# Batch 0 exchanged on the PE array instead of through DRAM, filter loads in one queue, and a new step plan for batches 1 to 7

## The chip, the cores and the metric

The kernel runs on one core of a Trainium2 chip. The metric is the device time of one execution in microseconds (us). Executions of one kernel on one chip mostly agree within about 1% (1.5% at most here); all comparisons below are between runs in the fast state, except where a run was made only once and its state is therefore unknown, which is said there.

## The reference

The input `x` (8 batches of 3072 rows and 256 channels) is filtered along its rows by a product in frequency space. The result goes through a max-out layer and an output projection.

```python
X = np.fft.rfft(x, axis=1)                       # x: 8 x 3072 x 256
y = np.fft.irfft(X * (filt_r + 1j * filt_i), n=3072, axis=1)
h = np.maximum(y @ w1, y @ w2)                   # w1, w2: 256 x 1024
out = h @ w_out                                  # w_out: 1024 x 256
```

The kernel does the transforms as matmuls, with 3072 = 128 x 24, in these stages for each batch:

- `f1`: a 128-point transform, `pa <- xb, C1`, evicted by ACT to `at`.
- an exchange of the partition axis with the 24 other rows: `at` is written to the DRAM tile `ad` and read back as `bt` (1.5 MB).
- `f2`, in eight groups: `px <- U, bt`, the product with the filter `F` on the DVE (`pq`), and `pz <- VP/VQ, pq`, evicted by ACT to `zt`.
- a second exchange through the DRAM tile `zd`, read back as `zr` in two halves.
- `s4` (`py <- zr, G1`), then the max-out layer (`ph`, `gt`) and the projection (`po`, `ot`), in 48 tiles of 8 steps each.

## The kernel before

Batch 0's transform stands before the loop of 384 steps (the setup). The transforms of batches 1 to 7 are put between the loop's steps by a plan. Max-out is computed as relu(y(w1-w2)) plus the linear part y w2 w_out, whose matrix `M` comes from `prep_w`.

```python
    def f1(b, c):
        ...
        TE.matmul(pa, C1, xb[b, c // 2][:, 2 * (c % 2):2 * (c % 2) + 2], start=True, stop=True)
        S.activation(at[:, 2 * (c % 2):2 * (c % 2) + 2], pa, AF.Copy)
        if c % 2 == 1:
            nc.sync.dma_start(out=ad[b][:, 2 * c - 2:2 * c + 2], in_=at)
    # ... setup ...
    load_f(8, 16, 0); load_f(8, 16, 1)             # written on two lines there
    G.memset(F[32:64, :, :, 0:8], 0.0)
    uu, mk = tables_u()
    for c in range(12):
        f1(0, c)
    f1_read(0)
    copy_f(8, 16, 0)
    copy_f(8, 16, 1)
    G.tensor_copy(hold, bt[0][0:1, 0:T:16, 0:1])   # POOL waits for bt here
    load_f(1, 8, 0)
    load_f(0, 8, 1)
    # ... f2 of batch 0, load_w, z_read(0, 1), prep_wd, z_read(0, 0), prep_w ...

    plan_f1(0, 1, range(3, 15), 17)     # f1 of batch 1 at these steps, its bt read at 17
    plan_x(0, 2, range(20, 48, 3))      # loads of x
    plan_f2(0, list(range(22, 39)), 33, 41)   # f2 of batch 1, zr halves read at 33 and 41
    # ... batches 2 to 4 ...
    for b in range(3, B):
        if b + 1 < B:
            plan_f2(b, list(range(0, 34, 2)), 19, 36)
        if b + 2 < B:
            plan_f1(b, b + 2, range(1, 25, 2), 28)
        if b + 3 < B:
            plan_x(b, b + 3, range(5, 48, 4))
```

## Time and profile before

The median of the first three runs was 601.76 us (600.74 to 604.93). The profiled execution took 596.9 us:

| Stage | from, to (us) | what bounds it |
|---|---|---|
| setup: batch 0's transform, weights | 0 to 82.4 (first `ph`) | transfers; PE busy 34.5 of 82.4 us |
| loop: 48 tiles, transforms of batches 1 to 7 | 82.4 to 592.5 (last store issued) | PE, busy 479.1 of 510.1 us, and waits for transfers |

The page of before cuts the span into 40 slices; each digit is the busy share of an engine in tenths, and `PEclk` is the granted TensorE clock.

```profile
PE   4415479797799998899699989998999989999996
ACT  5304237474466774575267646664676546555441
PEclk9955589899799999799799999999999999999998
DMA  8989466956369879669966974798147913551112
```

The first five slices are the setup: the DMA engines are busy, the PE hardly is, and its granted clock is 0.50 to 0.52 from 30 to 70 us. (The leading 9s of `PEclk` have no clock record behind them, the first record starts at 27.0 us: back-to-back 512-column matmuls at 23 to 27 us start 0.43 us apart, against 0.22 in the loop.)

The timeline of the DVE in the setup of before (start, duration, what; in brackets the idle time before it and what ended it):

```profile
39.87 3.48 DVE L402 TENSOR_TENSOR pq<-px,F 112x1024 bf16<-112x1024 f32 x3 [15.13 <-DMA F<-in_filt_r_dram]
...
56.77 0.60 DVE L259 TENSOR_SCALAR F<-F,e 48x256 bf16<-48x256 f32 x2
```

The first filter product waits 15 us for `F`. The second line is a small fix of the filter's first rows, 0.60 us for two instructions.

The list of what the PE waited for in the loop of before (total us, times, longest):

```profile
PE py L421 <- DMA zr<-zd: 18.9, 6, 6.2
PE pa L338 <- DMA xb<-in_x_dram: 5.0, 3, 4.2
PE px L392 <- DMA bt<-ad: 3.9, 3, 1.9
```

That is 27.8 us of idle PE. The clock records of the trace add 26.5 us at half clock inside the loop: the last 2.6 us of a stretch that began in the setup, and four stretches of 3.4 to 6.8 us that begin in or just after the longer of these waits (at 112.3, 149.8, 238.6 and 289.8 us).

The groups of before that evict `f1` and `f2` on ACT (count, busy us, mean ns of one):

```profile
L377 ACT ACTIVATE zt<-pz 112x512 bf16<-112x512 f32 x128 | 69.4, 595 | 72.0 <-PE pz L373 67.3
L339 ACT ACTIVATE at<-pa 128x512 bf16<-128x512 f32 x96 | 57.0, 600 | 35.4 <-PE pa L338 33.1
```

A 512-element eviction took 0.6 us (595 and 600 ns).

### The profile page before, as it was taken

To read this page: it belongs to the slowest core of one execution; us is meant where nothing else is said; L and a number is where in the kernel's file an instruction comes from. 1 tells how busy PE (TensorE), PEld (TensorE's weight loads), DVE (VectorE), ACT (ScalarE), POOL (GpSimd) and SP (SyncE) were. 2 spreads that over 40 slices of the span, in tenths; PEclk is the share of its full clock that TensorE was granted. 3 is DMA by queue.
4 is the path that set the end of the run, shared out by engine and by line. 5 is a ranking of instruction groups with operands and counts; after the bars stand their busy time and mean duration, and the time that the engine had idled before them with its cause. 6 is when DMAs were issued, how large, how long until landed. Compare 5 with 4: busy or idle time off the path is not lost.

```text
span 596.9 us, 11529 instructions
## 1 busy us (share of the span) xinstructions
PE 513.6 (86%) x4829; PEld 341.0 (57%) x4829; DVE 318.8 (53%) x415; ACT 324.5 (54%) x592; POOL 97.9 (16%) x148
## 2 busy tenths in 40 slices
PE   4415479797799998899699989998999989999996
PEld 0203236465466665566366656665666666677774
DVE  9426023493238736474177637773677467734342
ACT  5304237474466774575267646664676546555441
POOL 9863520110011001112011101110000000000000
PEclk9955589899799999799799999999999999999998
DMA  8989466956369879669966974798147913551112
GB/s 192 182 131 258 108 130 184 198 126 168 97 164 232 185 234 167 149 165 255 178 168 169 233 179 133 183 217 209 75 140 196 223 41 110 130 150 71 72 51 92
DMA packets 77736, 94.71 MB, mean 159 GB/s; under 512 B 5282, under 2 KB 57140, under 8 KB 76660
## 3 DMA queue, kind: packets, MB, share of 16 engines
q1 hardware_dynamic: 60196, 54.16, 39.4%
q0 software_dynamic: 17488, 39.81, 27.4%
q8 instruction: 38, 0.62, 0.4%
q14 instruction: 14, 0.11, 0.1%
HBM read 56.72 MB, written 50.33 MB: 179 GB/s over the span
## 4 chain that ended last, share of the span: by engine, by line
issue 52%; PE 21%; DMA 9%; POOL 5%; ACT 1%; DVE 0%; SPq 0%; POOLq 0%
PE ph L437 7%; PE po L462 7%; DMA zr<-zd 3%; DMA zd<-zt 3%; DMA xb<-in_x_dram 3%; POOL out_dram L468 3%; PE pa L338 2%; PE po L457 2%; PE pz L373 1%; POOL xb L89 1%; PE px L392 1%; PE py L421 1%; POOL Wd L302 1%; ACT zt L377 1%; POOL pq L402 0%
## 5 line engine op out<-in xcount | busy, mean ns | idle before, releaser
L442 ACT ACTIVATE gt<-ph 128x512 bf16<-128x512 f32 x298 | 176.3, 599 | 109.5 <-PE ph L437 108.7
L462 PE MATMUL po<-Wo,gt 128*128 128x256 bf16 x1536 | 232.9, 275 | 0.0
L462 PEld LDWEIGHTS <-gt 128*128 128x128 bf16 x1536 | 151.9, 99 | 60.1 <-issue 2.4
L402 DVE TENSOR_TENSOR pq<-px,F 112x1024 bf16<-112x1024 f32 x124 | 145.9, 1218 | 68.3 <-PE px L392 49.3
L464 DVE COPY ot<-po 128x512 f32<-128x512 f32 x96 | 66.0, 687 | 92.5 <-PE po L462 92.1
L377 ACT ACTIVATE zt<-pz 112x512 bf16<-112x512 f32 x128 | 69.4, 595 | 72.0 <-PE pz L373 67.3
L468 POOL DMA_DIRECT2D out_dram<-ot x48 | 25.8, 538 | 462.8 <-DVE ot L464 452.5
L437 PEld LDWEIGHTS <-Wd 128*128 128x128 bf16 x768 | 69.7, 99 | 29.5 <-issue 14.6
L440 DVE TENSOR_SCALAR gt<-ph 128x512 bf16<-128x512 f32 x86 | 59.0, 687 | 40.4 <-PE ph L437 32.4
L339 ACT ACTIVATE at<-pa 128x512 bf16<-128x512 f32 x96 | 57.0, 600 | 35.4 <-PE pa L338 33.1
L373 PE MATMUL pz<-pq,VP 48*64 48x256 bf16 x512 | 38.5, 288 | 30.6 <-DVE pq L402 15.2
L338 PE MATMUL pa<-xb,C 128*128 128x512 bf16 x96 | 38.6, 415 | 13.5 <-DMA xb<-in_x_dram 13.3
L421 PE MATMUL py<-G,zr 128*128 128x128 bf16 x384 | 30.4, 223 | 21.6 <-DMA zr<-zd 21.3
L421 PEld LDWEIGHTS <-zr 128*128 128x128 bf16 x384 | 25.6, 100 | 25.7 <-DMA zr<-zd 17.0
L373 PEld LDWEIGHTS <-VP 48*64 48x64 bf16 x512 | 19.1, 112 | 35.8 <-issue 32.9
L373 PE MATMUL pz<-pq,VQ 48*64 48x256 bf16 x512 | 36.7, 288 | 0.0
L392 PE MATMUL px<-bt,U 48*64 48x256 bf16 x512 | 29.7, 294 | 4.9 <-DMA bt<-ad 4.9
L89 POOL DMA_DIRECT2D xb<-in_x_dram x48 | 26.0, 555 | 0.7 <-issue 0.3
L392 PEld LDWEIGHTS <-U 48*64 48x64 bf16 x512 | 12.2, 110 | 17.9 <-issue 12.7
L338 PEld LDWEIGHTS <-C 128*128 128x128 bf16 x96 | 9.4, 101 | 21.1 <-DMA xb<-in_x_dram 10.9
L373 PEld LDWEIGHTS <-VQ 48*64 48x64 bf16 x512 | 18.7, 113 | 0.0
L402 POOL TENSOR_TENSOR pq<-xs,F 112x1024 bf16<-112x1024 f32 x4 | 8.5, 2136 | 4.1 <-ACT xs L401 2.8
(338 smaller groups left out, 525.8 us busy)
## 6 DMA issues: line engine op xcount, KB each, us to landing
out_dram<-ot POOLq DMA_DIRECT2D x48, 512.0 KB, 3.9
xb<-in_x_dram POOLq DMA_DIRECT2D x48, 256.0 KB, 6.7
ad<-at SPq DMA_DIRECT2D x48, 256.0 KB
bt<-ad SPq DMA_DIRECT2D x32, 384.0 KB
zd<-zt SPq DMA_DIRECT2D x64, 192.0 KB
zr<-zd SPq DMA_DIRECT2D x16, 768.0 KB
F<-F SPq DMA_DIRECT2D x6, 192.0 KB
w1f<-in_moe_w_dram SPq DMA_DIRECT2D x1, 1024.0 KB
```

What stands on the lines that cost most here:

```text
L338: TE.matmul(pa, C1, xb[b, c // 2][:, 2 * (c % 2):2 * (c % 2) + 2], start=True, stop=True)
L339: S.activation(at[:, 2 * (c % 2):2 * (c % 2) + 2], pa, AF.Copy)
L373: TE.matmul(pz[c][64 * k:64 * k + 64, i], W[64 * c:64 * c + 48, 2 * g + i, k], pq[k][64 * c:64 * c + 48, ri, i], start=(ri == 0), stop=(ri ...
L377: S.activation(zt[0:ROWS, c, o:o + 2], pz[c][0:ROWS], AF.Copy)
L392: TE.matmul(px[k][64 * c:64 * c + 64, i], U[64 * k:64 * k + 48, t_], bt_[64 * k:64 * k + 48, t_], start=True, stop=True)
L402: E.tensor_tensor(pq[k][0:ROWS], src[0:ROWS].rearrange("p (o i) d -> p o i d", o=1).to_broadcast([ROWS, 2, 2, D]), F[0:ROWS, :, k, 2 * g:2 ...
L421: TE.matmul(py[:, n], zr[b][:, 4 * i + n, 128 * dc:128 * dc + 128], G1, start=True, stop=True)
L437: TE.matmul(ph, Wd[:, dc, 128 * j:128 * j + 128], y_[:, dc].rearrange("p a b -> p (a b)"), start=(dc == 0), stop=(dc == 1))
L440: V.tensor_scalar(gt[tt][:, j], ph, 0.0, None, OP.max)
L442: S.activation(gt[tt][:, j], ph, AF.Relu)
L462: TE.matmul(p_, g_[:, jj, 128 * n:128 * n + 128], Wo[:, jj], start=False, stop=(jj == 7))
L464: V.tensor_copy(ot[tt][:, n - 1:n + 1], po[tt])
```

## The change

The intent: batch 0 has nothing to overlap with, so its two exchanges through DRAM stand open in the setup. The PE array can transpose instead: `f1` of batch 0 is computed with channels on partitions (`At`), transposed to `bt`, and after `f2`, which now also leaves channels on partitions (`Zt`), transposed again to `zr`. With no `bt` to wait for, all loads of `F` go out behind the loads of `x` without holds or memsets. `prep_w` moves into the loop, and batches 1 to 7 get new steps, counted over the whole loop.

```diff
+    def first_s1(c):
+        for dh in range(2):
+            pa = ps.tile([128, 4, 128], FP32, tag="ps", name="pa")
+            for n in range(4):
+                TE.matmul(pa[:, n], xb[0, c][:, n, 128 * dh:128 * dh + 128], C1, start=True, stop=True)
+            S.activation(At[:, dh, :, 4 * c:4 * c + 4].rearrange("p k n -> p n k"), pa, AF.Copy)
+    def first_t1(g, engines):      # transposes At to bt
...
+    def first_s3(g, pq, Zt):
+        ...                        # 32 matmuls of 48 columns into pz
+            S.activation(Zt[:, :, :, k0:k0 + 8].rearrange("p h n k -> p h k n"),
+                         pz[c].rearrange("p h i k (a n) -> p h (i k a) n", a=2), AF.Copy)
+    def first_t2(j, engine, Zt):   # transposes Zt to zr
...
-    G.memset(F[32:64, :, :, 0:8], 0.0)
-    for c in range(12):
-        f1(0, c)
-    f1_read(0)
-    G.tensor_copy(hold, bt[0][0:1, 0:T:16, 0:1])
...
+    plan(5, prep_w)
+    plan_f1(1, spaced(2, 1, 12), 15)
+    plan_f2(1, spaced(21, 2.5, 9), 34, 43)
...
+    plan_f1(3, spaced(68, 2, 12), 92)
+    plan_f2(3, spaced(98, 4, 9), 117, 132)
+    plan_x(4, spaced(88, 4, 6))
+    plan_f1(4, spaced(110, 2, 12), 134)
+    plan_f2(4, spaced(142, 4.5, 9), 163, 180)
+    for n in range(5, B):
+        o = 48 * (n - 5)
+        plan_x(n, spaced(124 + o, 4, 6))
+        plan_f1(n, spaced(148 + o, 2, 12), 172 + o)
+        plan_f2(n, spaced(182 + o, 5, 9), 204 + o, 224 + o)
```

`spaced(first, gap, count)` lists steps; the last numbers of a `plan_f1` and a `plan_f2` line are the steps of the `bt` read and of the two `zr` reads.

More of the change, by code (lines that the diff above doesn't have):

```diff
@@ L78 @@
     zrpool = ctx.enter_context(tc.tile_pool(name="zrpool", bufs=2))
+    late = ctx.enter_context(tc.tile_pool(name="late", bufs=1))
+    w2b = late.tile([128, 2, HID], BF16)
+    w2T = late.tile([128, 8, D], BF16)
     setup = ExitStack()
@@ L116, in copy_f @@
                               in_=F[64 * c:64 * c + 24, ri, :, u0:u1])
-    F0 = init.tile([48, 2, 2, D], FP32)
+            if c == 0:
+                nc.sync.dma_start(out=F[48:64, ri, :, u0:u1], in_=F[0:16, ri, :, u0:u1])
+    F0 = init.tile([64, 2, 2, D], FP32)
     def load_f0():
         for ri, f in enumerate((filt_r, filt_i)):
-            for q in range(2):
-                for dr in range(2):
-                    src = bass.AP(f.tensor, f.offset + 64 * dr * D, [[128 * D, J], [(96 - 128 * dr) * D, 2], [1, D]])
-                    if dr:
-                        src = bass.AP(f.tensor, f.offset + 64 * D, [[128 * D, J], [-32 * D, 2], [1, D]])
-                    p0 = 24 * q + 12 * dr
-                    nc.sync.dma_start(out=F0[p0:p0 + 12, ri], in_=src)
+            for p0, n in ((0, J), (12, J), (24, J), (36, J), (48, J), (60, 4)):
+                if p0 % 24 == 0:
+                    src = bass.AP(f.tensor, f.offset, [[128 * D, n], [96 * D, 2], [1, D]])
+                else:
+                    src = bass.AP(f.tensor, f.offset + 64 * D, [[128 * D, n], [-32 * D, 2], [1, D]])
+                nc.sync.dma_start(out=F0[p0:p0 + n, ri], in_=src)
     def patch_f0():
@@ L156 @@
            allow_small_or_imprecise_dtypes=True)
-    G.memset(F[32:64, :, :, 8:16], 0.0)
     V.memset(I128, 0.0)
@@ L223, in tables_u @@
         ub = init.tile([128, 2, 2, J], FP32)
-        uu = init.tile([128, 2, T, 2, J], FP32)
-        ru = init.tile([128, 2, T, 2, J], FP32)
+        ur = init.tile([128, 2, 2, T, 2, J], FP32, tag="uz", name="ur")
+        uu, ru = ur[:, 0], ur[:, 1]
         for q in range(2):
@@ L258, in fix_f @@
         for ri in range(2):
-            V.tensor_scalar(F[0:48, ri, 0, 0], F0[:, ri, 0], e0[0:48, ri:ri + 1], None, OP.mult)
-        V.tensor_copy(F[0:48, :, 1, 0], F0[:, :, 1])
+            V.tensor_scalar(F[0:64, ri, 0, 0], F0[:, ri, 0], e0[0:64, ri:ri + 1], None, OP.mult)
+        V.tensor_copy(F[0:64, :, 1, 0], F0[:, :, 1])
     def tables_pe():
@@ L281, in tables_pe @@
                 V.tensor_copy(VQ[:, 4 * k:4 * k + 4], pw)
-    w1f = init.tile([128, 2, HID], FP32)
-    w2f = init.tile([128, 2, HID], FP32)
-    w2b = init.tile([128, 2, HID], BF16)
-    w2T = init.tile([128, 8, D], BF16)
     def load_w():
-        nc.sync.dma_start(out=w1f, in_=moe_w1.rearrange("(c p) j -> p c j", p=128))
-        nc.sync.dma_start(out=w2f, in_=moe_w2.rearrange("(c p) j -> p c j", p=128))
+        w1f = init.tile([128, 2, 2, HID], FP32, tag="aw", name="wf")
+        for i, w in enumerate((moe_w1, moe_w2)):
+            G.dma_start(out=w1f[:, i], in_=w.rearrange("(c p) j -> p c j", p=128))
+        return w1f[:, 0], w1f[:, 1]
     def spin(n):
@@ L296, in spin, with prep_wd @@
             TE.matmul(pd, SW, VP[:, 0:4].rearrange("p u b n -> p (u b n)"), start=True, stop=True)
-    def prep_wd():
+    def prep_wd(w1f, w2f):
         for dc in range(2):
@@ L386, in gen_f2 @@
         made = []
-        for n, g in enumerate((4, 5, 6, 7, 2, 3, 1, 0)):
+        for g in (4, 5, 6, 7, 2, 3, 1, 0):
             px = [ps.tile([128, 2, D], FP32, tag="ps", name="px") for _ in range(2)]
@@ L396, in gen_f2 @@
                 pq.append(pqpool.tile([128, 2, 2, D], BF16, tag="pq", name="pq"))
-                E, src = V, px[k]
-                if b == 0 and k == 1 and n in (1, 3, 4, 6):
-                    E = G
-                    src = init.tile([128, 2, D], FP32, tag="xs", name="xs")
-                    S.activation(src[0:ROWS], px[k][0:ROWS], AF.Copy)
-                E.tensor_tensor(pq[k][0:ROWS],
-                                src[0:ROWS].rearrange("p (o i) d -> p o i d", o=1).to_broadcast([ROWS, 2, 2, D]),
+                V.tensor_tensor(pq[k][0:ROWS],
+                                px[k][0:ROWS].rearrange("p (o i) d -> p o i d", o=1).to_broadcast([ROWS, 2, 2, D]),
                                 F[0:ROWS, :, k, 2 * g:2 * g + 2], OP.mult)
@@ L411, in gen_f2 @@
         yield
+    def first_s1(c):
[5 more added lines that the diff above has]
+    def first_t1(g, engines):
+        for c in range(2):
+            t0 = 8 * (g // 2) + 4 * c + 2 * (g % 2)
+            pt = ps.tile([128, 2, D], FP32, tag="ps", name="pt")
+            for i in range(2):
+                for dh in range(2):
+                    k0 = 24 * 4 * (t0 + i)
+                    a_ = At[:, dh].rearrange("p k n -> p (k n)")
+                    TE.matmul(pt[0:64, i, 128 * dh:128 * dh + 128], a_[:, k0:k0 + 64], I128, start=True, stop=True)
+                    TE.matmul(pt[64:112, i, 128 * dh:128 * dh + 128], a_[:, k0 + 48:k0 + 96], I128,
+                              start=True, stop=True)
+            if engines[c] == "v":
+                V.tensor_copy(bt[0][0:ROWS, t0:t0 + 2], pt[0:ROWS])
+            else:
+                S.activation(bt[0][0:ROWS, t0:t0 + 2], pt[0:ROWS], AF.Copy)
@@ new lines, in first_s2 @@
+    def first_s2(g, pool):
+        px = [ps.tile([128, 2, D], FP32, tag="ps", name="px") for _ in range(2)]
+        for i in range(2):
+            for k, c in QUADS:
+                t_ = 8 * (g // 2) + 4 * c + 2 * (g % 2) + i
+                TE.matmul(px[k][64 * c:64 * c + 64, i], U[64 * k:64 * k + 48, t_],
+                          bt[0][64 * k:64 * k + 48, t_], start=True, stop=True)
+        pq = []
+        for k in range(2):
+            pq.append(pqpool.tile([128, 2, 2, D], BF16, tag="pq", name="pq"))
+            E, src = V, px[k]
+            if k == 1 and pool:
+                E = G
+                src = init.tile([128, 2, D], FP32, tag="xs", name="xs")
+                S.activation(src[0:ROWS], px[k][0:ROWS], AF.Copy)
+            E.tensor_tensor(pq[k][0:ROWS],
+                            src[0:ROWS].rearrange("p (o i) d -> p o i d", o=1).to_broadcast([ROWS, 2, 2, D]),
+                            F[0:ROWS, :, k, 2 * g:2 * g + 2], OP.mult)
+        return pq
@@ new lines, in first_s3 @@
+    def first_s3(g, pq, Zt):
+        pz = [ps.tile([128, 2, 2, 2, 48], FP32, tag="ps", name="pz") for _ in range(2)]
+        for dh in range(2):
+            for i in range(2):
+                for k in range(2):
+                    for ri, W in enumerate((VP, VQ)):
+                        for c in range(2):
+                            TE.matmul(pz[c][:, dh, i, k], pq[k][64 * c:64 * c + 48, ri, i, 128 * dh:128 * dh + 128],
+                                      W[64 * c:64 * c + 48, 2 * g + i, k, 0:48], start=(ri == 0), stop=(ri == 1))
+        for c in range(2):
+            k0 = 4 * (8 * (g // 2) + 4 * c + 2 * (g % 2))
+            S.activation(Zt[:, :, :, k0:k0 + 8].rearrange("p h n k -> p h k n"),
+                         pz[c].rearrange("p h i k (a n) -> p h (i k a) n", a=2), AF.Copy)
@@ L413 @@
+    def first_t2(j, engine, Zt):
+        pt = ps.tile([128, 2, D], FP32, tag="ps", name="pt")
+        for n in range(2):
+            for dh in range(2):
+                TE.matmul(pt[:, n, 128 * dh:128 * dh + 128], Zt[:, dh, 2 * j + n], I128, start=True, stop=True)
+        if engine is V:
+            V.tensor_copy(zr[0][:, 2 * j:2 * j + 2], pt)
+        else:
+            S.activation(zr[0][:, 2 * j:2 * j + 2], pt, AF.Copy)
     yt = {}
@@ L438, in moe_h @@
                       y_[:, dc].rearrange("p a b -> p (a b)"), start=(dc == 0), stop=(dc == 1))
-        if j in (1, 5) and not (tt < 12 and 20 <= 8 * (tt % 6) + j < 40):
+        if j in (1, 5) and not in_f2(8 * tt + j):
             V.tensor_scalar(gt[tt][:, j], ph, 0.0, None, OP.max)
@@ L478 @@
     load_f(8, 16, 1)
-    G.memset(F[32:64, :, :, 0:8], 0.0)
-    uu, mk = tables_u()
-    for c in range(12):
-        f1(0, c)
-    patch_f0()
-    f1_read(0)
-    copy_f(8, 16, 0)
-    copy_f(8, 16, 1)
-    hold = init.tile([1, 2, 1], BF16)
-    G.tensor_copy(hold, bt[0][0:1, 0:T:16, 0:1])
     load_f(1, 8, 0)
     load_f(0, 8, 1)
-    load_wo()
+    At = init.tile([128, 2, 128, N2], BF16, tag="aw", name="At")
+    bt[0] = bpool.tile([128, T, D], BF16, tag="bt", name="bt")
+    for c in range(6):
+        first_s1(c)
+    uu, mk = tables_u()
+    patch_f0()
+    for c in range(2):
+        copy_f(8, 16, c)
     copy_f(1, 8, 0)
     copy_f(0, 8, 1)
+    first_t1(4, "vv")
+    first_t1(5, "vv")
     sines_u(uu, mk)
     tables_pe()
-    spin(8)
-    f2 = gen_f2(0)
-    for n in range(8):
-        if n == 7:
-            fix_f()
-        next(f2)
-        if n == 2:
-            load_w()
-        if n == 5:
-            z_read(0, 1)
-            prep_wd()
-    drain(f2)
-    z_read(0, 0)
-    prep_w()
-    spin(16)
+    Zt = init.tile([128, 2, N2, 128], BF16, tag="uz", name="Zt")
+    for g in (6, 7, 2, 3, 1, 0):
+        first_t1(g, "sv")
+    wf = load_w()
+    load_wo()
+    pend = None
+    for n, g in enumerate((4, 5, 6, 7, 2, 3, 1, 0)):
+        if n == 6:
+            fix_f()
+        pq = first_s2(g, n in (0, 2, 3, 5))
+        if pend:
+            first_s3(*pend, Zt)
+        pend = g, pq
+        if n == 4:
+            prep_wd(*wf)
+    first_s3(*pend, Zt)
+    zr[0] = zrpool.tile([128, N2, D], BF16, tag="zr", name="zr")
+    for c in range(6):
+        load_x(1, c)
+    for j in range(4):
+        first_t2(j, (V, S)[j % 2], Zt)
+    for j in range(4, 12):
+        first_t2(j, (V, S)[j % 2], Zt)
     setup.close()
@@ L515, with plan, plan_x, plan_f1 @@
     opool = ctx.enter_context(tc.tile_pool(name="opool", bufs=2))
-    keep = ctx.enter_context(tc.tile_pool(name="keep", bufs=1))
-    hold = keep.tile([1, 2, 1], BF16)
-    G.tensor_copy(hold, zr[0][0:1, 0:2, 0:1])
-    for c in range(6):
-        load_x(1, c)
     s4(0)
     todo = {}
-    def plan(b, step, fn, *a):
-        todo.setdefault((b, step), []).append((fn, a))
-    def plan_f1(b, nb, steps, read):
-        for c, n in zip(range(12), steps):
-            plan(b + n // 48, n % 48, f1, nb, c)
-        plan(b + read // 48, read % 48, f1_read, nb)
-    def plan_f2(b, steps, z1, z0):
+    def plan(step, fn, *a):
+        todo.setdefault(step, []).append((fn, a))
+    def plan_x(n, steps):
+        for c, s_ in enumerate(steps):
+            plan(s_, load_x, n, c)
+    def plan_f1(n, steps, read):
+        for c, s_ in enumerate(steps):
+            plan(s_, f1, n, c)
+        plan(read, f1_read, n)
+    def plan_f2(n, steps, z1, z0):
         g = []
@@ L540, in go, with spaced, in_f2 @@
             if not g:
-                g.append(gen_f2(b + 1))
+                g.append(gen_f2(n))
             next(g[0], None)
-        for n in list(steps[1:16:2]) + [steps[16]]:
-            plan(b, n, go)
-        plan(b, z1, z_read, b + 1, 1)
-        plan(b, z0, z_read, b + 1, 0)
-    def plan_x(b, nb, steps):
-        for c, n in zip(range(6), steps):
-            plan(b, n, load_x, nb, c)
-    plan_f1(0, 1, range(3, 15), 17)
-    plan_x(0, 2, range(20, 48, 3))
-    plan_f2(0, list(range(22, 39)), 33, 41)
-    plan_f1(1, 2, range(0, 12), 15)
-    plan_x(1, 3, range(17, 48, 3))
-    plan_f2(1, list(range(20, 37)), 31, 39)
-    plan_f1(1, 3, range(38, 50), 53)
-    plan_x(2, 4, range(7, 40, 3))
-    plan_f2(2, [n for n in range(9, 48) if n % 3], 23, 37)
-    plan_f1(2, 4, [n for n in range(14, 48) if n % 3], 41)
-    plan_x(2, 5, range(26, 48, 4))
-    for b in range(3, B):
-        if b + 1 < B:
-            plan_f2(b, list(range(0, 34, 2)), 19, 36)
-        if b + 2 < B:
-            plan_f1(b, b + 2, range(1, 25, 2), 28)
-        if b + 3 < B:
-            plan_x(b, b + 3, range(5, 48, 4))
+        for s_ in steps:
+            plan(s_, go)
+        plan(z1, z_read, n, 1)
+        plan(z0, z_read, n, 0)
+    def spaced(first, gap, count):
+        return [first + int(gap * i) for i in range(count)]
+    plan(5, prep_w)
+    plan_f1(1, spaced(2, 1, 12), 15)
+    plan_f2(1, spaced(21, 2.5, 9), 34, 43)
+    plan_x(2, spaced(16, 2.5, 6))
+    plan_f1(2, spaced(31, 1.2, 12), 46)
+    plan_f2(2, spaced(57, 3, 9), 71, 83)
+    plan_x(3, spaced(50, 3, 6))
+    plan_f1(3, spaced(68, 2, 12), 92)
[8 more added lines that the diff above has]
+        plan_f2(n, spaced(182 + o, 5, 9), 204 + o, 224 + o)
+    def in_f2(step):
+        return 20 <= step < 43 or 57 <= step < 83 or 98 <= step < 132
     for tt in range(6 * B + 1):
@@ L574 @@
         for j in range(8):
-            step = 8 * i + j
+            step = 8 * tt + j
             if tt < 6 * B:
@@ L579 @@
                 moe_o(tt - 1, j)
-            for fn, a in todo.get((b, step), ()):
+            for fn, a in todo.get(step, ()):
                 fn(*a)
```

## The prediction

> **What bounds it now.** Two stages. Setup (batch 0's transform, weights) lasts until the first `ph` matmul at 82.4 us (timeline). The TensorE is mostly idle there (windows: 0 us busy in 30-40, 1.7 in 60-70), its clock 0.5 from 30 to 75 us; it waits for transfers. The DVE waits 15.1 us for `F` (to 39.9): its loads are held back behind two 7 us POOL memsets and a `hold` copy that waits for `bt` (31.0). POOL waits 5.6 us for `w2f`, so its last `pq` is done at 68.3 and the PE waits 11 us for it. Then zd write 3.3 and zr read 5.8 us stand in the chain, until 81.2.
> The loop (82.4 to 592.5, 510 us) is PE-bound: a plain tile takes 8.2 us, one with transform work about 10.9, so I estimate 48*8.2+7*10.5 = 467 us, so some 40 us are stalls: `zr` waits 18.9 us, `xb` 5.0, `bt` 3.9 (list of waits), each long one followed by 3.4 to 6.8 us at half clock (windows: 0.67 to 0.83 near 110, 150, 240, 290).
>
> **What the change does, costed.**
> Removed in setup: four DRAM crossings of batch 0 (1.5 MB each), both memsets (13.9 us POOL; the first also held the DVE), holds, spins.
> Added on PE: 128 + 48 transposes at about 0.12 us on half clock (the 16 `w2b` transposes took 1.89 us): `t2` 5.7 us, `t1` 6 to 11; `s3` becomes 256 narrow matmuls. Evictions: 16 for `t1`, 12 for `t2`, about 0.65 us each, shared by DVE and ACT.
> New chain, estimated: x landed 13.5; `At` 15; tables 21; `t1` until 28-31. `F` loads queue right behind x: twelve at 0.57 us each on POOL, so the half for the first groups lands near 20, its copies near 25-28. First `pq` near 31 (39.9 before). Groups at 2.3 us. The weights' buffer is shared with `At`, so they load only after `t1` and land near 40; casts and subtraction (2.0+4.6 us POOL) still precede POOL's last `pq`, near 50. Then `t2`, `s4`: first `ph` near 63 (58 to 70). Gain about 18 us.
> Moved: `prep_w` into the loop (step 5): +3 us, before hidden behind the zr read.
>
> **Loop.** x(4) is issued about 20 steps before use: the 4.2 us stall at 237-241 and its cold clock go, -7. The last group of batches 5 to 7 comes 16 steps before its `py` (14 before): three waits of about 2 us go, -6. Batch 3: same distance, less bunched, -3. Against: batch 1's last group comes at step 41, not 38, before a `py` at 47: its zr wait (6.2 us) grows, +2. Sum -11 with prep_w.
>
> [...] The new setup stays mostly at half clock.
>
> **Predicted: 573 us, 8 in 10 between 560 and 588.** Faster by over 2%: 0.92; within 2%: 0.07; slower: 0.01.
>
> **What would show it.** First `pq` before 34 us; first `ph` at 58-70; no ad/zd traffic for batch 0; PE waits for POOL `pq` before `t2`; the longest loop wait is `zr` of batch 1; no `xb` wait over 1 us; no `zr` wait in batches 5 to 7.
>
> **What would make it wrong.** `F` copies or weights landing late because everything shares one queue; narrow `s3` or `t1` costing more at half clock; batch 1's or 2's zr wait growing past 10 us.

About 18 us in the setup and 11 in the loop, off the 602 us of before, give the 573. What the trace of before shows is clock records of 3.41 us and multiples of it, at half clock for 44.4 us in the setup and for 3.4 to 6.8 us in or just after the longer waits of the loop. "Mostly at half clock" was the estimate for the new setup; in the changed kernel the records show half clock from 49.8 to 83.9 us and do not begin before 43.0.

## More of the kernel before

The timeline of the SP queue of before, around the end of one batch in the steady part of the loop:

```profile
394.18 0.98 SPq L382 DMA_DIRECT2D zd<-zt  x2
396.78 5.36 SPq L348 DMA_DIRECT2D bt<-ad  x4
402.18 3.31 SPq L382 DMA_DIRECT2D zd<-zt  x2
412.03 0.45 SPq L355 DMA_DIRECT2D zr<-zd  x1
```

The `zr` read must wait until the last `zd` writes have landed (in the loop of before the SP queue waits 70.4 us for `zd` ahead of its `zr` reads, in 22 waits). Here it goes 6.5 us after the last of them was issued (402.18+3.31 to 412.03). Just ahead of them stand four issues that read the next batch's `bt`.

## The result

The changed kernel took 624.89 us (median of 4, 622.9 to 626.01) against 603.02 for before on the same chip: a ratio of 1.036, 95% interval 1.031 to 1.041. It is slower. Ratios here and below are the mean time of one kernel's runs over that of the other's of the same rounds, so they are not quite the ratio of the medians quoted. Executions over 1.5% slower than the fastest of the same kernel are left out of the means. The profiled executions, 624.2 and 596.9 us, differ by a little more than the medians do.

| (us, from the profiles) | before | after | predicted |
|---|---|---|---|
| first `pq` on the DVE | 39.9 | 45.3 | 31 |
| first `ph` (end of setup) | 82.4 | 86.1 | 63 |
| first `ph` to the last store | 510.1 | 533.7 | 499 |

So both halves of the prediction failed: the setup is 3.7 us longer, not 19 shorter, and the loop 23.6 us longer, not 11 shorter.

The same lines of the page of after:

```profile
PE   3164379898899959994899969996799989999996
ACT  7977977486367727781476527663377545555541
PEclk9995589899799979998899979999799989999999
DMA  9955513967976795678647954688445943341112
```

The DMA engines are indeed less busy in the setup (slices 3 to 6 add up to 16 tenths, where before they add up to 27), but ACT is now the engine that is busy there. Its groups show why:

```profile
L463 ACT ACTIVATE Zt<-pz 128x384 bf16<-128x384 f32 x16 | 28.2, 2110 | 5.8 <-PE pz L459 5.8
L414 ACT ACTIVATE At<-pa 128x512 bf16<-128x512 f32 x12 | 28.3, 2835 | 2.2 <-PE pa L413 2.2
```

The twelve `At` evictions have the shape of the old 0.6 us ones and take 28.3 us together, one every 2.36 us (the mean of one, 2.8 us, includes the overlap with its neighbour). The sixteen of `Zt` take 28.2 us. At 0.6 us each, all 28 would be about 17 us; some 40 us of ACT time were added, on the chain that leads to `ph`. The timeline of the PE where the setup ends:

```profile
80.27 4.58 PE L470 MATMUL pt<-I,Zt 128*128 128x128 bf16 x48 [5.49 <-ACT Zt L463]
86.07 1.45 PE L500 MATMUL ph<-y__1099,Wd 128*128 128x512 bf16 x6 [0.77 <-ACT y__1099 L487]
```

The last transposes wait for `Zt`, and the first `ph` follows. A smaller surprise stands in the timeline of the DVE of after, in answer to the 0.60 us line above:

```profile
63.37 5.75 DVE L262 TENSOR_SCALAR F<-F,e 64x256 bf16<-64x256 f32 x2
```

Those two small instructions now take 5.75 us. The first of them (3.6 us) ends as POOL's weight subtraction ends (62.2 to 66.8 us), the second (2.2 us) as POOL's next `pq` product ends (66.8 to 69.0 us).

The list of the PE's waits in the loop of after:

```profile
PE py L484 <- DMA zr<-zd: 23.1, 4, 10.1
PE px L392 <- DMA bt<-ad: 20.2, 5, 9.0
```

The waits for `xb` are gone as predicted, but the sum rises from 27.8 to 43.3 us, and the time at half clock inside the loop, summed from the clock records, from 26.5 to 47.8 us. The extra waiting is 15.5 us and, as an estimate, the slower clock can cost up to half of 21.3 us, about 10.7: together enough for the 23.6.

Most of the rise is in the waits for `bt` (3.9 to 20.2 us); those for `zr` rise by 4.2. The `bt` waits are those of batches 1, 3 and 4 (2.55, 6.74 and 10.95 us). A `bt` read must wait until the `ad` writes have landed. What the SP queue waited for in the loop, first of before, then of after (total us, times, longest):

```profile
SPq L348 <- DMA ad<-at: 10.4, 8, 1.6
SPq L348 <- DMA ad<-at: 27.8, 8, 8.2
```

For batch 4 the new plan puts the `bt` read 2 steps behind the step of the last `ad` write (132 and 134), where before had 10 (127 and 137). In the trace of after that write is issued at 282.7 us and the read at 291.6, and the first `px` of batch 4, 8 steps after the read, waits 8.97 us.

The timeline of the SP queue of after, around the longest single wait, for the `zr` of batch 5:

```profile
412.02 3.27 SPq L348 DMA_DIRECT2D bt<-ad  x4
415.38 4.08 SPq L382 DMA_DIRECT2D zd<-zt  x2
435.21 0.45 SPq L355 DMA_DIRECT2D zr<-zd  x1
```

The new plan put the `bt` read of the next batch (step 220) immediately ahead of the last `zd` writes of this one (step 222). The `zr` read can go only 15.8 us after the last `zd` issue (415.38+4.08 to 435.21), where it took 6.5 us in the lines of before. `py` then waits 10.13 us (6.4 and 5.5 us in the two other kernels with this plan, below). In the lines of before, too, a `bt` read stands just ahead of the `zd` writes, so its place alone does not explain why 6.5 became 15.8. The trace of after has one thing more there: four loads of `x`, 256 KB each, are issued between 416.6 and 427.3 us, where before issues none between 392 and 412 us.

### The profile page after: what moved, and what is told of

Same layout as the page of the kernel before. It is cut to its first block, busy times and chain, and to the rows that moved or that the text cites. A ratio compares the mean times of both kernels' runs of the same rounds, so it can differ in the third digit from the quotient of the medians.

```text
span 624.2 us, 12146 instructions
## 1 busy us (share of the span) xinstructions
PE 519.8 (83%) x5145; PEld 352.3 (56%) x5145; DVE 319.8 (51%) x420; ACT 377.6 (60%) x615; POOL 84.6 (14%) x146
## 4 chain that ended last, share of the span: by engine, by line
PE 40%; issue 32%; DMA 11%; ACT 9%; POOL 5%; DVE 2%; SPq 0%; POOLq 0%; ACTq 0%
PE ph L500 14%; PE po L525 13%; ACT At L414 5%; DMA bt<-ad 4%; DMA zd<-zt 3%; PE po L520 3%; PE pz L373 2%; PE pa L338 2%; PE px L392 2%; DMA zr<-zd 2%; ACT Zt L463 2%; PE py L484 2%; DMA ad<-at 2%; POOL out_dram L531 2%; DVE pq L397 1%
## 5 line engine op out<-in xcount | busy, mean ns | idle before, releaser
L505 ACT ACTIVATE gt<-ph 128x512 bf16<-128x512 f32 x309 | 183.2, 600 | 130.2 <-PE ph L500 129.3
L397 DVE TENSOR_TENSOR pq<-px,F 112x1024 bf16<-112x1024 f32 x112 | 131.8, 1218 | 63.4 <-PE px L392 62.6
L377 ACT ACTIVATE zt<-pz 112x512 bf16<-112x512 f32 x112 | 60.7, 594 | 45.0 <-PE pz L373 42.5
L503 DVE TENSOR_SCALAR gt<-ph 128x512 bf16<-128x512 f32 x75 | 51.3, 684 | 29.5 <-PE ph L500 28.6
L392 PE MATMUL px<-bt,U 48*64 48x256 bf16 x448 | 25.3, 292 | 20.2 <-DMA bt<-ad 20.2
L338 PE MATMUL pa<-xb,C 128*128 128x512 bf16 x84 | 32.0, 381 | 0.0
L463 ACT ACTIVATE Zt<-pz 128x384 bf16<-128x384 f32 x16 | 28.2, 2110 | 5.8 <-PE pz L459 5.8
L414 ACT ACTIVATE At<-pa 128x512 bf16<-128x512 f32 x12 | 28.3, 2835 | 2.2 <-PE pa L413 2.2
L373 PE MATMUL pz<-pq,VP 48*64 48x256 bf16 x448 | 28.6, 275 | 0.0
L373 PE MATMUL pz<-pq,VQ 48*64 48x256 bf16 x448 | 28.2, 272 | 0.0
L459 PE MATMUL pz<-VP,pq 48*128 48x48 bf16 x128 | 7.1, 209 | 14.1 <-POOL pq L447 9.5
```

Of the source, the lines that this page charges most:

```text
L373: TE.matmul(pz[c][64 * k:64 * k + 64, i], W[64 * c:64 * c + 48, 2 * g + i, k], pq[k][64 * c:64 * c + 48, ri, i], start=(ri == 0), stop=(ri ...
L377: S.activation(zt[0:ROWS, c, o:o + 2], pz[c][0:ROWS], AF.Copy)
L392: TE.matmul(px[k][64 * c:64 * c + 64, i], U[64 * k:64 * k + 48, t_], bt_[64 * k:64 * k + 48, t_], start=True, stop=True)
L397: V.tensor_tensor(pq[k][0:ROWS], px[k][0:ROWS].rearrange("p (o i) d -> p o i d", o=1).to_broadcast([ROWS, 2, 2, D]), F[0:ROWS, :, k, 2 * g ...
L414: S.activation(At[:, dh, :, 4 * c:4 * c + 4].rearrange("p k n -> p n k"), pa, AF.Copy)
L503: V.tensor_scalar(gt[tt][:, j], ph, 0.0, None, OP.max)
```

## The experiments

Theory S: the setup lost its gain to ACT writing single 2-byte elements far apart. Theory P: the loop lost by the step plan itself, and in it theory Q: by `bt` reads issued just ahead of `zd` writes that someone waits for. The rivals are L (the loop suffers from the new setup), R (any stride costs as much) and D (the number of steps is too small, whatever lies between). Every run gave the right result. The medians are in us; runs of one block shared a chip.

| run | median | ratio to before (95%) | first `ph` | loop |
|---|---|---|---|---|
| old plan, new setup | 602.82 | 1.011 (1.006-1.016) | 86.8 | 512.1 |
| new plan, old setup | 623.30 | 1.044 (1.038-1.050) | 81.5 | 534.6 |
| run-writing evictions | 609.01 | 1.022 (1.016-1.028) | 69.7 | 532.5 |
| | | | | |
| old plan and run-writing | 583.85 | 0.977 (0.963-0.991) | 67.7 | 508.1 |
| run-writing, plan shifted | 584.29 | 0.974 (0.963-0.985) | 67.6 | 511.4 |
| `At` alone writes runs (one run, state unknown) | 611.32 | - | 74.4 | 530.7 |
| version A: shifted further, setup reordered | 573.66 | 0.956 (0.949-0.964) | 63.0 | 503.3 |
| | | | | |
| old plan, run-writing, `bt` read later | 572.17 | 0.956 (0.951-0.961) | 68.5 | 497.6 |
| A with batch 4's read earlier | 562.78 | 0.941 (0.937-0.946) | 62.0 | 493.5 |
| A with the weights' loads later | 570.05 | 0.953 (0.948-0.957) | 61.3 | 500.4 |

"First `ph`" and "loop" are read from each run's profile as above. The intervals of 1.022, 0.977 and 0.974 exclude 1, but not a difference under 2%.

### The plan and the setup, each alone

Edit of the first run (the changed kernel with the old steps, counted over the whole loop):

```diff
-    plan_f1(1, spaced(2, 1, 12), 15)
-    plan_f2(1, spaced(21, 2.5, 9), 34, 43)
...
+    old_f1(0, 1, range(3, 15), 17)
+    old_f2(0, list(range(22, 39)), 33, 41)
...
```

> The changed kernel with the step plan of before put back (batches 1 to 7), its new setup kept. Theory P (the new step plan alone lengthens the loop, by lining up the bt and zr reads of neighbouring batches just ahead of their use): the time from the first ph to the last out falls from about 534 us to about 513 (510 of before plus about 3 for prep_w in the loop), and the whole to about 604 us. Rival L (the loop is longer because of what the new setup leaves behind: prep_w inside it, other buffers, x(1) loads): it stays near 620 to 625 us.

Edit of the second (the kernel before with the new steps, `prep_w` left in the setup):

```diff
-    plan_f1(0, 1, range(3, 15), 17)
-    plan_f2(0, list(range(22, 39)), 33, 41)
...
+    plan_f1(1, spaced(2, 1, 12), 15)
+    plan_f2(1, spaced(21, 2.5, 9), 34, 43)
...
```

> The kernel before with only the new step plan, its own setup kept. Theory P: about 20 to 24 us slower than before, 622 to 627 us, with the same waits for bt (batches 1, 3, 4) and zr (batches 1, 4, 5, 6) as in the changed kernel. Rival L: within 5 us of before, 600 to 606 us.

Measured: with the old plan the loop takes 512.1 us (513 expected), with the new plan on the old kernel 534.6 (24.5 more than before). Theory P holds and L falls: the loop's loss is the plan's, whichever setup precedes it. The second run also has the waits of the changed kernel, 23.8 us for `bt` and 20.2 for `zr`. (With the plan goes the list of steps, `in_f2`, at which ACT evicts `ph` in place of the DVE.) The first run also shows what the new setup is worth by itself, with nothing else changed but `prep_w` in the loop: about 1% slower.

### The evictions

```diff
-            S.activation(At[:, dh, :, 4 * c:4 * c + 4].rearrange("p k n -> p n k"), pa, AF.Copy)
+            S.activation(At[:, dh, :, 4 * c:4 * c + 4], pa.rearrange("p n k -> p k n"), AF.Copy)
...
-            S.activation(Zt[:, :, :, k0:k0 + 8].rearrange("p h n k -> p h k n"),
-                         pz[c].rearrange("p h i k (a n) -> p h (i k a) n", a=2), AF.Copy)
+            S.activation(Zt[:, :, :, k0:k0 + 8],
+                         pz[c].rearrange("p h i k (a n) -> p h n (i k a)", a=2), AF.Copy)
```

The same elements go to the same places. Only the order of walking changed: the write now has 4 or 8 neighbours in a row, and PSUM is read with a stride.

> The changed kernel with its two re-ordering evictions (At, Zt) walked in the other order: the same elements, but the write now goes in runs of 4 and 8 adjacent bf16 elements and the PSUM side is read with a stride. Theory S (the 2.4 and 1.8 us of these evictions come from writing single 2-byte elements 48 and 256 bytes apart): they fall to about 0.6 us, about 35 us of ACT time go, the first ph comes at 65 to 72 us instead of 86, the whole at 604 to 612 us. Rival R (any stride on either side costs as much, so reading PSUM with a stride is no better): evictions stay at 1.8 us or more, the time stays at 620 to 626 us.

The groups of the run-writing kernel:

```profile
L463 ACT ACTIVATE Zt<-pz 128x384 bf16<-128x384 f32 x16 | 7.0, 488 | 26.6 <-PE pz L459 26.6
L414 ACT ACTIVATE At<-pa 128x512 bf16<-128x512 f32 x12 | 6.5, 594 | 5.7 <-PE pa L413 5.6
```

`At` is back at 0.59 us and `Zt` at 0.49; 43.0 us of ACT time are gone (56.5 to 13.5), and the first `ph` comes 16.4 us sooner. Theory S holds and R falls. The loop did not move (532.5), as it should not.

With the `At` edit alone:

> The changed kernel where only the At eviction writes runs, Zt still writes single elements. The At chain then ends near 16 us instead of 34.6, but the first pq waits for F until about 35 us instead of about 43, and the 16 Zt evictions of 1.8 us still bind the groups. I expect the first ph at 76 to 80 us (86 in the changed kernel, 69.7 with both), so that each of the two evictions is worth about half of the 16 us.

The first `ph` came at 74.4, a little sooner than I expected: `At`, repaired first, is worth 11.7 of the 16.4 us, not half. Its chain ran alone (the PE waited for it 13 us in the changed kernel), whereas part of the `Zt` work was hidden beside other waits.

The probe appended 26 evictions of 256 elements to the kernel before, for instance

```diff
+        S.activation(pb[:, 0:256], pp[:, 0:256], AF.Copy)             # L593
+        S.activation(pb[:, 0:512:2], pp[:, 0:256], AF.Copy)           # L595
+        S.activation(pb[:, 0:1024:4], pp[:, 0:256], AF.Copy)          # L597
+        S.activation(pb[:, 0:2048:8], pp[:, 0:256], AF.Copy)          # L599
+        S.activation(pb[:, 0:6144:24], pp[:, 0:256], AF.Copy)         # L601
+        S.activation(pb3[:, 0:128, 0:2], ..., AF.Copy)                # L603, pairs in a pitch of 24
+        S.activation(..., pp.rearrange(...)[:, 0:64], AF.Copy)        # L611, PSUM read at a stride of 128
+        S.activation(pf[:, 0:512:2], pp[:, 0:256], AF.Copy)           # L615, fp32
+        S.activation(pf[:, 0:1024:4], pp[:, 0:256], AF.Copy)          # L617, fp32
```

> The kernel before with 26 forms of a 256-element eviction appended at its end, first on ACT, then on DVE, each twice: bf16 written at strides of 1, 2, 4, 8 and 24 elements, in runs of 2, 4 and 8 inside a 24-element pitch, PSUM read at strides of 2 and 128, and fp32 written at strides of 1, 2 and 4. Outputs stay right. [...] Rival W (any 2-byte write that is not next to the last one is slow): bf16 stride 2 is already slow and fp32 strides are all fast. On the DVE I expect the same pattern.

The groups of the probe (the mean time of one is the number after the comma; the state of this single run is unknown, so its forms are compared only with each other):

```profile
L593 ACT ACTIVATE pr<-pp 128x256 bf16<-128x256 f32 x2 | 0.8, 383 | 4.6 <-PE po L462 4.6
L595 ACT ACTIVATE pr<-pp 128x256 bf16<-128x256 f32 x2 | 0.9, 455 | 0.1
L597 ACT ACTIVATE pr<-pp 128x256 bf16<-128x256 f32 x2 | 1.5, 736 | 0.1
L599 ACT ACTIVATE pr<-pp 128x256 bf16<-128x256 f32 x2 | 2.6, 1300 | 0.1
L601 ACT ACTIVATE pr<-pp 128x256 bf16<-128x256 f32 x2 | 2.7, 1342 | 0.1
L603 ACT ACTIVATE pr<-pp 128x256 bf16<-128x256 f32 x2 | 0.8, 392 | 0.1
L611 ACT ACTIVATE pr<-pp 128x256 bf16<-128x256 f32 x2 | 0.8, 384 | 0.1
L615 ACT ACTIVATE pf<-pp 128x256 f32<-128x256 f32 x2 | 0.8, 395 | 0.1
L617 ACT ACTIVATE pf<-pp 128x256 f32<-128x256 f32 x2 | 1.2, 618 | 0.1
L627 DVE CAST pr<-pp 128x256 bf16<-128x256 f32 x2 | 2.7, 1331 | 0.1
```

A bf16 write costs almost nothing extra when neighbours come in pairs (0.39 us inside a pitch of 24) and rises when single elements lie apart: 0.74 us at 8 bytes, 1.30 at 16, 1.34 at 48, against 0.38 contiguous. Reading PSUM at a stride of 512 bytes cost nothing on ACT (0.384 against 0.383 us). The DVE shows the same (1.33 us at the stride of 24, last line; 0.72 at 8 bytes, 1.29 at 16, 0.43 in pairs, against 0.43 contiguous), so moving these evictions to it would probably not have helped (not run). Rival W was not quite right: for bf16 a stride of 2 is nearly free (0.46 us) and only from a stride of 4 on is it slow (0.74), and fp32 is not fast at every stride (0.40 us at 8 bytes, 0.62 at 16, against 0.38 contiguous). Why the times rise as they do is not shown.

### Both repairs together

> The changed kernel with both repairs: the old step plan and the evictions that write runs. If the two causes are independent, the savings add: 603 us of the old plan alone, less the 16 us by which the first ph came sooner with runs, so 585 to 590 us, about 2% faster than before. If they are not (the loop starts sooner but waits longer for the same transfers), 595 us or more.

583.85 us: the two savings add as independent causes should, and this is the first version faster than before, by 2.3% (interval 0.9 to 3.7%).

### What in the plan costs

```diff
-    plan_x(4, spaced(88, 4, 6))
-    plan_f1(4, spaced(110, 2, 12), 134)
+    plan_x(4, spaced(76, 4, 6))
+    plan_f1(4, spaced(98, 2, 12), 122)
...
-        plan_x(n, spaced(124 + o, 4, 6))
-        plan_f1(n, spaced(148 + o, 2, 12), 172 + o)
+        plan_x(n, spaced(112 + o, 4, 6))
+        plan_f1(n, spaced(136 + o, 2, 12), 160 + o)
```

> The run-writing kernel with the new step plan, where only x loads, forward transforms and the bt read of batches 4 to 7 come 12 steps earlier; all f2 groups and zr reads stay at their steps. Theory Q (the bt read of the next batch is put on the queue just before the last zd writes of this one, which then wait behind its 1.5 MB): the zr waits of batches 4 and 5 (about 6 and 6 to 10 us) vanish though their own steps did not move, and so does the bt wait of batch 4 (about 10 us); the time falls from 609 to about 580 us. Rival D (the distances from the last group to py, 12 and 16 steps, are simply too short for a write and a read of a DRAM tile): the zr waits of batches 4 and 5 stay, only the bt wait of batch 4 goes, about 597 us.

The loop fell by 21 us to 511.4, and the time to 584.29 (about 580 expected). The `zr` wait of batch 4 went from 5.97 to 1.47 us and that of batch 5 from 5.52 to nothing, though no `f2` group and no `zr` read had moved. That speaks for Q against D. It does not single out the `bt` read, because the loads of `x` and the forward transforms moved with it. The `bt` wait of batch 4, 12.3 us in the run-writing kernel, vanished too, which D expected as well: its read now stands 20 steps ahead of its first use instead of 8. The `bt` wait of batch 3, whose read had not moved, stayed (9.3 and 10.4 us). One wait is new: `zr` of batch 3, 6.35 us. The shift had put batch 4's `bt` read (step 122) 8 steps ahead of batch 3's last `zd` writes (step 130), and their reader could go only 11.3 us after them; the collision had moved.

The test that changes one number is made on the kernel with the old plan, where the `bt` read of the later batches stood at step 28 of 48, between the `zd` writes, and now follows the last `zr` read at 36:

```diff
-            old_f1(b, b + 2, range(1, 25, 2), 28)
+            old_f1(b, b + 2, range(1, 25, 2), 38)
```

> The kernel with the old plan and run-writing evictions, where only the step of the bt read changes, for the batches read from batch 3's loop on: after the last zr read (38) instead of before the last zd writes (28); its own first use stays 12 steps away. Theory Q (a bt read just ahead of the last zd writes delays them): the zr waits of the last three boundaries (3.3, 2.8 and 2.1 us) go below 0.5 us, and the time falls by 6 to 9 us, 584 to about 577. Rival D (distance alone): they stay, no change, 582 to 586 us.

The timeline of the SP queue at the same place of the loop, first with the read at 28, then with the read at 38:

```profile
379.61 4.56 SPq L348 DMA_DIRECT2D bt<-ad  x4
385.07 3.01 SPq L382 DMA_DIRECT2D zd<-zt  x2
394.95 0.45 SPq L355 DMA_DIRECT2D zr<-zd  x1
```

```profile
372.70 8.94 SPq L382 DMA_DIRECT2D zd<-zt  x4
384.72 0.45 SPq L355 DMA_DIRECT2D zr<-zd  x1
385.28 6.30 SPq L348 DMA_DIRECT2D bt<-ad  x4
```

From the last `zd` issue to the `zr` read it was 6.9 us and is now 3.1. The last three `zr` waits (3.25, 2.77 and 2.14 us) are gone, and the ratio to before goes from 0.977 to 0.956, about 12 us and more than the 6 to 9 expected (the two ran on different chips; the loops differ by 10.5 us in the profiles). Theory Q holds for these batches and D falls, since nothing but the read moved.

### A version faster than both

The next kernel takes the shifted plan, moves batch 3's forward transform as well, and reorders the setup:

```diff
-    plan_f1(3, spaced(68, 2, 12), 92)
+    plan_f1(3, spaced(60, 2, 12), 86)
...
-        if n == 6:
-            fix_f()
-        if n == 4:
+        if n == 5:
             prep_wd(*wf)
...
+    fix_f()
     first_t1(4, "vv")
```

> The shifted plan with three more moves: batch 3's forward transform 8 steps and its read 6 steps earlier, fix_f before the first transposes (in the run-writing kernel it took 6 us beside POOL's weight subtraction, 1 us in the kernel before), and the weight casts after POOL's last pq. I expect the first ph at 63 to 66 us, no bt wait for batch 3 over 2 us, and 562 to 575 us in all.

573.66 us, with the first `ph` at 63.0. Batch 3's `bt` wait, with 4 steps from the last `ad` write to the read and 12 from there to the first use (2 and 6 before the move), fell from 10.4 to 2.8 us. The filter fix now runs at 16 us, before POOL has arithmetic to do:

```profile
15.89 0.36 DVE L262 TENSOR_SCALAR F<-F,e 64x256 bf16<-64x256 f32 x1 [2.82 <-DMA F<-in_filt_r_dram]
16.64 0.34 DVE L262 TENSOR_SCALAR F<-F,e 64x256 bf16<-64x256 f32 x1 [0.40 <-issue]
```

In the changed kernel the same two instructions took 5.75 us beside POOL's work and ended where POOL's instructions ended; without it they took 0.70 us. What held them up beside POOL was not shown.

The remaining `zr` wait of batch 3 (6.51 us) was then tested by moving batch 4 alone (its loads of `x`, forward transform and read):

```diff
-    plan_x(4, spaced(76, 4, 6))
-    plan_f1(4, spaced(98, 2, 12), 122)
+    plan_x(4, spaced(68, 4, 6))
+    plan_f1(4, spaced(90, 2, 12), 115)
```

> The best kernel so far, with only batch 4's x loads, forward transform and bt read 7 to 8 steps earlier, so that this read is 15 steps ahead of batch 3's last zd writes instead of 8. In the run before, those writes were issued at 251 to 253.6 us, 2.4 us behind the bt read (244.9 to 248.7), and their zr read could go only at 263.8. Theory Q: write to zr read falls from about 11 us to 5 or 6, the zr wait of batch 3 (6.5 us) to under 2, and the time from 573.7 to about 566. Rival D: the wait stays at 5 to 6.5 us, no change.

562.78 us, 5.9% faster than before and the best. Batch 3's `zr` wait fell to 2.73 us (under 2 expected), and the time from its last `zd` issue to the `zr` read from 10.2 to 7.3 us (5 or 6 expected). In the loop of this kernel the PE waits 11.9 us for `zr` and `bt` together, against 43.3 in the changed kernel:

```profile
PE py L484 <- DMA zr<-zd: 8.2, 3, 4.6
PE px L392 <- DMA bt<-ad: 3.7, 2, 2.2
```

Last, a miss:

```diff
-    wf = load_w()
-    load_wo()
     pend = None
...
         pend = g, pq
+        if n == 0:
+            wf = load_w()
+            load_wo()
```

> The best kernel so far, with only the weights' loads issued after POOL's first pq instead of before it. The second half of F is copied at 30 to 36 us while the 2.5 MB of weights move, and the DVE waits until 46.4 us for it. If the weights' traffic holds those copies back, that wait ends near 41 us, the first ph comes 3 to 5 us sooner (63.0 to about 59), and the time is about 570 us. If the copies are late for another reason, the DVE still waits to 46 us and the weights only land later: no gain or a loss of 2 to 4 us.

The DVE still waited for the second half of `F` until 45.57 us (46.35 without this edit), and the first `ph` came at 61.3, against 62.0 for the kernel with the same setup, without this edit, on the same chip. The run does not clear the weights, though. Their loads were issued at 34.8 to 36.4 us instead of 30.4 to 31.8 (the kernel on the same chip), and the last copy of `F` at 36.0, so the two still overlapped. What holds those copies back is left open.

## Why the prediction was wrong

**The evictions of the exchange (wrong, and the step that failed in the setup).** The prediction priced the evictions of the transposes, "Evictions: 16 for `t1`, 12 for `t2`, about 0.65 us each, shared by DVE and ACT", and that was right: they took 0.60 us on ACT and 0.69 on the DVE. What it did not price are the evictions that re-order, 12 of `At` and 16 of `Zt`, whose counts happen to be the same the other way round. They stand in it only as "`At` 15" and "Groups at 2.3 us", which fits evictions of about 0.6 us, as those of `at` and `zt` were, but no slower ones. They took 2.36 and about 1.8 us each, 56.5 us in all, and `At` was ready at 34.6 us instead of 15. With the write order turned, the first transpose of `At` starts at 15.8 us, as predicted, and the first `ph` came at 69.7 instead of 86.1: this term is 16.4 of the 23 us by which the setup was missed.

**The rest of the setup chain (sizes off).** "First `pq` near 31" was 35.5 in the run-writing kernel and 32.3 after the reordering. The 5.75 us that the filter fix takes beside POOL were not foreseen. With it, and the weight casts, moved out of the way the first `ph` was at 63.0; that this is the number predicted is in part luck, since the setup that reached it is not the one that was costed. The new setup as a whole (exchange on the PE, loads of `F` without holds, `prep_w` in the loop) is thus worth about 19 us once repaired; its parts were not timed apart. What was feared instead, narrow matmuls at half clock that cost more than estimated, did not happen: in the changed kernel `t1` kept the PE busy for 6.3 us (6 to 11 predicted), `t2` for 4.6 (5.7), and `s3` for 7.6, where the 128 wider ones of before took 10.9.

**The loop (wrong, and the larger failure).** The sum "-11" has no term for `bt`, whose waits grew by 16.3 us, more than the whole rise: the new steps left 2 steps between the last `ad` write and the read, and 6 to 8 from there to the first use. Moved earlier, the `bt` wait of batch 4 vanished (12.3 us in the kernel it was tested on) and that of batch 3 fell from 10.4 to 2.8. For `zr` the sum was built from the distance in steps between a group and its reader: "The last group of batches 5 to 7 comes 16 steps before its `py` (14 before): three waits of about 2 us go". The distance did grow, and yet batch 5's wait grew from 2.74 us in the kernel before to 10.1 in the changed one (6.4 and 5.5 in the others with this plan). Beside its last `zd` writes the new plan puts the `bt` read of the next batch, two steps ahead, and loads of `x`. Moving these and the forward transforms 12 steps earlier takes the wait away; which of the three does it was shown only for the `bt` read, and in the old plan. The prediction listed steps of one batch and never set two neighbouring batches side by side on the SP queue. The plan alone costs 24.5 us, and that one shift wins back 21.

**Batch 1 (wrong).** Its `zr` wait was called the longest of the loop and expected to grow from 6.2 us; it was 4.6. The longest were batch 5's `zr` (10.1) and batch 4's `bt` (9.0).

**The waits for `xb` (right).** The 4.2 us stall and all others for `xb` are gone. **`prep_w` (not settled).** The loop with the old plan is 2 us longer than before, 3 were predicted; but with the evictions repaired and the same plan it is 2 us shorter (508.1), so 3 us cannot be told from other differences. **Batch 0's traffic (right).** The page lists 42 writes of `ad` for 48 and 56 of `zd` for 64.

**Open.** That a `bt` read just ahead delays the `zd` writes is shown by moving it, in the old plan. Whether they wait in the order of the queue or only share bandwidth with it is not: no run here separates the two. The two first runs also do not add up exactly: +1.1% and +4.4% alone, +3.6% together. Part of that may be the difference between chips (before itself was between 593 and 605 us).

## What to carry to other kernels

Price an eviction by how it writes as well as by its shape: if a copy re-orders 2-byte elements, walk it so that at least pairs of neighbours are written together (256 bf16 elements took 0.39 us in pairs, 1.34 singly at the same pitch of 48 bytes), and let the PSUM side have the stride (0.384 us against 0.383 without). When transfers of several batches share a queue, lay the batches side by side and look at what stands just ahead of each transfer that someone is about to wait for; a large read that is not urgent belongs behind it (with a 1.5 MB read just ahead, two `zd` writes let their reader go 6.5 to 15.8 us after their last issue, the longest with four loads of `x` there too; with the read behind them, in the old plan, after 3.1). Count the steps from a write to the read of the same data as well as from the read to its first use. A plan and a mechanism that change together should be timed apart before either is judged.
